# Pieces of 256 and 320 tokens instead of 320 and 256 in the first two batches of a fused attention and squared-relu layer

## The chip, the cores and the metric

The kernel runs on one core of a Trainium2 chip. The metric is the device time of one execution in microseconds (us); less is better. A core has five engines with queues of their own, each of which runs its instructions strictly in its order: TensorE (PE: matmuls, with PEld for loading their weights), VectorE (DVE), ScalarE (ACT), GpSimd (POOL) and SyncE (SP). They wait for each other through semaphores. Transfers between the main memory and the core's memory are issued by POOL and SP here, and run on 16 DMA engines. Matmuls write to PSUM, eight banks of 2 KB per partition; ACT and DVE read it from there.

## The reference

```python
def sm_attn(qq, kk, vv):
    s = scale * np.matmul(qq, kk.transpose(0, 1, 3, 2))
    s = s - np.max(s, axis=-1, keepdims=True)
    a = np.exp(s)
    a = a / (np.sum(a, axis=-1, keepdims=True) + 1e-09)
    return np.matmul(a, vv)
p_packed = sm_attn(p, k, v)
out = sm_attn(q, p_packed, p_packed)
...
x = np.ascontiguousarray(attn_out.transpose(0, 2, 1, 3)).reshape(B * S, H * D)
h = x @ w_in
r = np.maximum(h, 0.0)
g = r * r
return (g @ w_out).astype(np.float32)
```

There are 8 batches of 8 heads, 576 tokens and a head size of 64; p has 32 rows per head. So the first attention packs 576 rows of k and v into 32 rows (softmax one, over 576), and the second one lets 576 rows of q look at those 32 (softmax two, over 32). What comes out, 4608 tokens of 512 values, passes a first layer of 512 x 2048, a relu that is squared, and a second layer of 2048 x 512. Everything is float32 outside; the kernel computes in bfloat16 with float32 sums.

## The kernel before, in words

Nothing here is ordered by a compiler or a planner at build time. One long text, `ORDER` (L50), names every step as a word, and `run` (L770) issues the steps in that order; each step puts its instructions at the end of its engine's queue. A letter behind a colon gives the engine where there is a choice: `v` is DVE, `a` ACT, `p` POOL. DVE is meant where none is given.

The heads of a batch are worked on as two quads, 0 and 1. With b for the batch and q for the quad, the words of one batch are, in the order in which they depend on each other:

- `Lkbq`, `Lvbq`, `Lq`/`LA`/`LB`: loads of k, v and q, issued by POOL (L270, L310 and others). In batches 0 and 1, q comes in two parts, A and B. `Wi`, `Wo`: the two weights, in pieces, also by POOL. POOL's loads have eight semaphores in turn, so that a load waits until the eighth one before it has landed, and what stands behind it on POOL waits too. `pf`, `P0`, `P1`: p of the first two batches, loaded by SP, cast and turned by DVE (L233, L237).
- `kT` (DVE, L353) turns k; `s1` (PE, L377) gives the scores of softmax one; `m1` its maximum (DVE, L403); `x1` the exponential (ACT, L415); `eT` turns it on PE (L435), `eo` copies that out of PSUM; `rd`, `pv` (PE, L459) and `pp` (DVE, L472) make the packed rows; `bd` (DVE) and `pt`, `po` turn them for the next two uses.
- `qT`, or `qA` and `qB` (DVE, L365): q turned. `s2`, or `zA` and `zB` (PE, L377): scores of softmax two. `t2`/`tA`/`tB` (DVE, L520): turned out of PSUM so that 32 neighbours are one row; `m` maximum (L525); `s` difference (L531); `x` exponential (ACT, L537); `u` sum and reciprocal (DVE, L543, L545); `a` product with it (L551); `aT`/`TA`/`TB` (DVE, L565): turned for the first layer.
- `w0`, `w1`, and in batch 0 `wa` and `wb` for the halves of `w0` (PE, L576): the packed rows times the first layer's weights, so that the first layer is applied to the 32 packed rows once, and each token needs only its mixture of them. `W..` (L421, L423): copied out of PSUM.
- `hb.p.f` (PE, L592): the first layer of batch b, piece p of its tokens, block f of 16 blocks of 128 features: two matmuls, one for each quad, into one bank. `r` (ACT L597, DVE L599): relu out of that bank. `qb.p.f`, with f up to 7 (DVE L637, ACT L635, POOL): the square, two blocks at once, into `gT`.
- `ot.j` (PE, L650): the second layer of 128 tokens (t is 0 to 35), two of its 16 matmuls at a step. `c` copies the 128 x 512 result out of PSUM, `d` stores it (SP, L681).
- `Zn` (L337): n matmuls of 288 columns of zeros, of which nothing is used. They stand only in the first stretch, where PE has nothing else to do.

PSUM is shared out by hand: two double banks (`psa`) for scores, turns and `w`; four more, first as three `spare` and one `idle`, then, from the first `h` on, as two `x` and two `y`. A step that takes one of two buffers waits for the reader of the step before the last that took it. In batch 0, `h` of an even block takes `x`, of an odd block `y`; the `o` of the first two token tiles takes `y`, later ones `x`.

Batches 2 to 7 pass softmax two in one go and the first layer in halves of 288. Batches 0 and 1 pass both in the two pieces that `CUTS` gives:

```python
PIECES = range(2)
HALVES = ((0, HALF), (HALF, S))
CUTS = ((0, 320), (320, S))
...
def part(self, b, hf):
    return (CUTS if b in PIECES else HALVES)[hf]
...
def span(self, hf):
    s0, s1 = (0, S) if hf is None else CUTS[hf]
    return slice(s0 // NP, s1 // NP)
```

So `h0.0.f` and `zA0` work on the first piece, `h0.1.f` and `zB0` on the second. Token tiles 0 and 1 (tokens 0 to 255) lie within the first piece, tiles 2 and 3 (256 to 511) reach into or lie in the second.

Of the kernel before, what the change touches and what calls it, by code (L numbers as in the profile page):

```python
# [24 lines left out]
S = T * NP  # L25
# [14 lines left out]
CUTS = ((0, 320), (320, S))  # L40
# [10 lines left out]
pf Lk00 Lk01 Lv00 LA0 Lv01 Wi11 P0 Wi10 kT00 I Z30 s100 Wi00 LB0 kT01 P1 Wi01 m100 Z7 s101 Wi21 x100 m101 x101 Z6 eT00  # L51
Wi20 qA01 Z4 eT01 qA00 eo00:a eo01:v Lk10 rd0 Z5 pv0 pp0 bd0 Z4 pt0 Lk11 zA0 po0:v tA01 tA00 Z12 wb00 mA01 Wb00:a mA00
Z2 wb01 sA01:p Wb01:v Wo0 sA00:v xA01 uA01 xA00 Lv11 qB00 qB01 aA01:p uA00 Z21 zB0 Lv10 tB01 Z1 wa00 tB00 aA00:p mB01
Wa00:a Z3 wa01 TA01 mB00 Wa01:a sB01:p TA00 sB00:v Z8 h0.0.8 xB01 h0.0.1 xB00 r0.0.8:v h0.0.0 Wo2 r0.0.1:a h0.0.3 uB01
r0.0.0:a h0.0.10 uB00 h0.0.11 aB01:p r0.0.10:a h0.0.2 r0.0.3:a q0.0.0:v r0.0.2:a h0.0.9 r0.0.11:v aB00:p q0.0.1:a TB01
w101 LA1 q0.0.5:v r0.0.9:a w100 TB00 W101:a W100:v h0.1.0 q0.0.4:p h0.1.1 h0.1.11 r0.1.0:a h0.1.10 r0.1.1:a kT10
h0.1.2 r0.1.10:a LB1 h0.1.3 r0.1.11:a h0.0.12 r0.1.2:a q0.1.0:v h0.1.15 r0.1.3:a q0.1.5:p h0.0.4 r0.0.12:v r0.1.15:a
h0.0.13 kT11 r0.0.4:a h0.1.6 h0.0.5 r0.0.13:a Wo1 h0.0.6 q0.1.1:v r0.1.6:a h0.1.13 q0.0.6:v r0.0.5:a s11 r0.1.13:v Wo3
q0.0.2:a r0.0.6:v h0.1.14 m110 h0.1.7 r0.1.14:a h0.1.12 Pr h0.1.9 r0.1.7:a h0.1.4 q0.1.7:v r0.1.12:a h0.0.15 r0.1.9:v
x110 h0.0.14 r0.1.4:v h0.0.7 m111 r0.0.15:a h0.1.8 eT10 r0.0.14:a r0.1.8:v h0.1.5 r0.0.7:a o2.0 eo10:v q0.1.3:a o3.0  # L60
r0.1.5:v x111 q0.0.3:v o1.0 q0.1.2:v o0.0 q0.1.4:a q0.0.7:v o0.1 rd1 q0.1.6:p eT11 o1.1 eo11:v o3.1 pv1 Lk20 o0.2 pp1
o1.2 bd1 o3.2 o1.3 qA10 pt1 qA11 o0.3 o3.3 po1:v zA1 qB11 w011 tA11 o2.1 W011:a tA10 o2.2 qB10 o2.3 mA11 mA10 w110
w111 sA11 o3.4 Lk21 W110:a sA10 o1.4 W111:v o0.4 xA11 o0.5 xA10 uA11 zB1 w010 tB11 o1.5 uA10 o1.6 aA11 W010:a o0.6
mB11 o1.7 aA10 o2.4 Px TA11 Lk30 c1:v o3.5 o0.7 TA10 sB11 o3.6 kT20 d1 c0:a h1.0.8 Lv20 o2.5 r1.0.8:a Pt h1.0.3 xB11
h1.0.6 tB10 d0 r1.0.3:a o2.6 Pu:v h1.0.1 r1.0.6:a Lv21 o2.7 r1.0.1:a kT21 h1.0.0 c2:a h1.0.2 o3.7 r1.0.0:a uB11 Lv30
d2 r1.0.2:a s12 q1.0.0:v c3:a h1.0.4 mB10 o4.0 m120 q1.0.1:a Lq2 h1.0.5 d3 o5.0 r1.0.4:a m121 r1.0.5:a o5.1 aB11 x120
h1.0.12 q1.0.2:v h1.0.7 o4.1 kT30 Lq3 x121 eT20 o4.2 TB11 r1.0.12:a r1.0.7:v o5.2 sB10 eo20:a h1.0.13 rd2 q1.0.3:v
eT21 xB10 r1.0.13:v h1.0.9 eo21:a o4.3 r1.0.9:v h1.0.15 q1.0.6:a uB10 pv2 q1.0.4:v h1.0.10 pp2 o5.3 Lv31 r1.0.15:a
r1.0.10:v o4.4 aB10 pt2 h1.0.14 bd2 h1.0.11 po2:v r1.0.14:a o5.4 bs2:v r1.0.11:a w121 TB10 w020 q1.0.5:v W121:a h1.1.8
q1.0.7:v h1.1.9 o4.5 W020:v o5.5 r1.1.8:a r1.1.9:a o4.6 Lv40 h1.1.4 qT21 h1.1.6 r1.1.4:a o5.6 q1.1.4:a qT20 o4.7 Lk31  # L70
r1.1.6:a h1.1.2 o5.7 c4:v h1.1.14 r1.1.2:a s22 c5:a r1.1.14:v h1.1.10 t221 o6.0 d5 r1.1.10:a h1.1.1 t220 o6.1 r1.1.1:a
h1.1.7 m221 o6.2 d4 h1.1.0 r1.1.7:a o6.3 qT30 r1.1.0:a h1.1.5 q1.1.3:a h1.1.3 q1.1.0:v Lq4 o6.4 qT31 r1.1.5:a o6.5
q1.1.2:a sb21:v h1.1.13 r1.1.3:a o8.0 m220 r1.1.13:a h1.1.11 o6.6 q1.1.1:a Lq5 r1.1.11:v o6.7 x221 sb20:v h1.1.15 o8.1
c6:a q1.1.5:v h1.1.12 x220 su21 d6 o7.0 r1.1.12:a Lk41 w120 r1.1.15:a w021 kT31 q1.1.6:a o7.1 q1.1.7:a o8.2 su20
W120:a o7.2 o8.3 a221 W021:a o7.3 a220 o8.4 o7.4 aT21 o8.5 aT20 o7.5 h2.0.2 h2.0.3 r2.0.2:v o7.6 Lk40 r2.0.3:a o8.6
q2.0.1 o7.7 h2.0.1 h2.0.0 r2.0.1:v o8.7 r2.0.0:a c7:v s13 c8:a q2.0.0 h2.0.7 d7 h2.0.6 m130 Lk50 r2.0.7:a o9.0
r2.0.6:a h2.0.4 m131 o10.0 d8 r2.0.4:a h2.0.9 q2.0.3 x131 h2.0.5 r2.0.9:v o10.1 r2.0.5:v x130 o9.1 kT41 h2.0.12
h2.0.10 r2.0.12:a q2.0.2 eT31 Lk51 r2.0.10:a eT30 rd3 h2.1.1 eo31:v h2.0.8 r2.1.1:a o9.2 kT40 r2.0.8:a h2.1.0 eo30:a
o9.3 r2.1.0:v h2.0.11 Lk60 q2.0.4 pv3 q2.1.0 r2.0.11:a h2.1.3 pp3 o10.2 r2.1.3:a q2.0.5 h2.0.13 bd3 o10.3 bs3:v
r2.0.13:a Lv41 h2.1.5 h2.0.14 r2.1.5:v s23 q2.0.6 o9.4 qT40 r2.0.14:a h2.0.15 o9.5 t231 r2.0.15:a h2.1.4 h2.1.8 q2.0.7  # L80
o10.4 Lv51 r2.1.8:a t230 o9.6 r2.1.4:a o10.5 m231 h2.1.7 h2.1.2 q2.1.2 o9.7 r2.1.7:a qT41 r2.1.2:a o10.6 c9:a sb31:v
h2.1.11 Lq6 h2.1.14 r2.1.11:a d9 o11.0 q2.1.1 h2.1.6 m230 r2.1.14:a o11.1 r2.1.6:a o10.7 x231 sb30:v h2.1.10 h2.1.12
q2.1.3 pt3 r2.1.10:a o11.2 c10:v po3:a h2.1.9 r2.1.12:a su31 w030 x230 w130 d10 o11.3 r2.1.9:a q2.1.5 W030:a o12.0
q2.1.4 h2.1.13 su30 o12.1 W130:a o11.4 a231 o12.2 r2.1.13:a w131 a230 w031 o12.3 W031:a aT31 o11.5 aT30 h2.1.15 W131:v
o12.4 r2.1.15:a h3.0.0 h3.0.11 r3.0.0:a o12.5 q2.1.6 q2.1.7 r3.0.11:a h3.0.1 s14 r3.0.1:v h3.0.3 kT51 h3.0.7 r3.0.3:a
o11.6 r3.0.7:a m140 h3.0.10 o11.7 r3.0.10:a q3.0.0 h3.0.8 x140 kT50 h3.0.2 o12.6 r3.0.8:a c11:v o12.7 Lk61 r3.0.2:a
h3.0.14 q3.0.5 h3.0.5 d11 m141 o14.0 r3.0.14:a c12:a eT40 q3.0.1 h3.0.4 r3.0.5:a o13.0 x141 r3.0.4:v Lk71 h3.1.9 d12
eo40:v o14.1 r3.1.9:a q3.0.2 o13.1 h3.0.12 rd4 h3.0.6 o13.2 r3.0.12:v r3.0.6:a o14.2 h3.0.13 q3.0.3 h3.1.8 eT41
r3.0.13:v o13.3 r3.1.8:a eo41:v h3.0.9 q3.0.6 h3.0.15 o14.3 q3.1.4 r3.0.9:a r3.0.15:v pv4 q3.0.4 h3.1.5 Lv50 pp4
h3.1.6 r3.1.5:a q3.0.7 o14.4 bd4 o13.4 bs4:v r3.1.6:a pt4 Lv60 o14.5 h3.1.1 h3.1.0 po4:v r3.1.1:a o14.6 r3.1.0:v  # L90
h3.1.14 q3.1.0 w041 r3.1.14:a w141 o14.7 W141:v h3.1.3 W041:a h3.1.2 o13.5 o13.6 r3.1.2:a r3.1.3:v c14:a s24 q3.1.1
h3.1.7 h3.1.4 t240 r3.1.7:a o15.0 d14 r3.1.4:a o13.7 t241 h3.1.10 c13:a o15.1 q3.1.3 r3.1.10:a h3.1.12 q3.1.2 o17.0
m240 r3.1.12:a o17.1 d13 m241 h3.1.11 h3.1.13 r3.1.11:a o15.2 sb40:v r3.1.13:a h3.1.15 o15.3 q3.1.5 r3.1.15:a sb41:v
o17.2 x240 o17.3 q3.1.7 o15.4 x241 q3.1.6 su40 w140 w040 o15.5 W040:a su41 o17.4 o15.6 W140:a a240 o17.5 o15.7 a241
s15 c15:a aT40 o17.6 aT41 o16.0 m150 d15 h4.0.4 h4.0.10 kT60 r4.0.4:a o16.1 r4.0.10:a h4.0.0 m151 x150 o17.7 Lk70
h4.0.1 r4.0.0:v o16.2 x151 qT50 o16.3 r4.0.1:a h4.0.3 c17:v eT50 r4.0.3:a h4.0.2 q4.0.0 eo50:a o16.4 d17 r4.0.2:v
h4.0.7 rd5 qT51 o18.0 r4.0.7:a h4.0.11 q4.0.1 o16.5 Lq7 r4.0.11:a kT61 h4.0.6 h4.0.5 o18.1 r4.0.6:a q4.0.5 o16.6
r4.0.5:a q4.0.3 h4.0.13 q4.0.2 h4.0.12 r4.0.13:v eT51 o16.7 eo51:v r4.0.12:a h4.0.15 o18.2 q4.0.6 r4.0.15:a h4.0.9
c16:v h4.1.0 o18.3 r4.0.9:a r4.1.0:v d16 pv5 h4.1.1 Lv61 h4.0.8 o19.0 pp5 r4.1.1:a o19.1 r4.0.8:v h4.0.14 Lv70 q4.1.0
h4.1.3 bd5 r4.0.14:a pt5 o19.2 q4.0.4 bs5:a po5:v h4.1.2 r4.1.3:v o18.4 r4.1.2:a q4.0.7 h4.1.5 q4.1.1 h4.1.15 o18.5  # L100
r4.1.5:v o18.6 r4.1.15:a h4.1.10 h4.1.4 s25 r4.1.10:v r4.1.4:a o18.7 qT61 h4.1.8 c18:a h4.1.7 t251 o19.3 o20.0 q4.1.2
r4.1.8:a d18 o19.4 r4.1.7:a m251 h4.1.6 h4.1.14 t250 o19.5 r4.1.6:a o20.1 sb51:v r4.1.14:a h4.1.9 q4.1.3 w150 r4.1.9:a
w151 m250 x251 h4.1.13 o19.6 W150:v r4.1.13:a o20.2 W151:a o19.7 sb50:v h4.1.12 c19:a h4.1.11 w050 su51 w051 d19 x250
o20.3 r4.1.11:a q4.1.4 o21.0 W050:a q4.1.7 o21.1 q4.1.5 o20.4 su50 r4.1.12:a o21.2 W051:a o21.3 q4.1.6 o20.5 a250
o20.6 a251 o21.4 o20.7 aT50 aT51 s16 qT60 o21.5 c20:a h5.0.1 m160 h5.0.0 r5.0.1:a o21.6 r5.0.0:a m161 h5.0.3 d20
h5.0.2 r5.0.3:a o21.7 q5.0.0 x160 r5.0.2:v h5.0.4 o22.0 kT71 c21:a h5.0.7 eT60 r5.0.4:a q5.0.1 o23.0 r5.0.7:a kT70 d21
x161 h5.0.11 h5.0.5 eo60:v o22.1 r5.0.11:a r5.0.5:v eT61 rd6 h5.0.15 eo61:v o23.1 r5.0.15:a h5.0.9 q5.0.2 pv6 r5.0.9:v
# [29 lines left out]
class Kernel:  # L137
# [184 lines left out]
# [4 lines that stand above are left out]
# [64 lines left out]
    def st_s2(self, b, hf=None):  # L390
# [3 lines left out]
        for qd in range(self.NQ):  # L394
            t = self.att[b, qd]
            ps = t["ps_s2", hf] = self.turn32("ps_s2") if hf is None else one[:, qd:qd + 1]
            x.append((ps, t["ppd"], t["qT"], [(h, self.group(qd, h)) for h in range(QH)]))
        self.scores(HALVES if hf is None else CUTS[hf:hf + 1], x)

# [425 lines left out]
```

## Time and profile before

| what | us |
|---|---|
| median of three runs (243.95 to 244.98) | 244.84 |
| the profiled execution | 243.8 |
| span of the profile, first to last instruction | 242.0 |
| busy in it: TensorE, VectorE, ScalarE, GpSimd | 236.4, 206.3, 138.2, 75.9 |
| first useful first-layer matmul / first second-layer matmul | 21.89 / 33.52 |
| last matmul's result ready to be copied | 234.00 |
| mean relu of 256, 288, 320 elements on ACT | 0.390, 0.411, 0.442 |
| the same on DVE | 0.418, 0.453, 0.481 |
| mean square of 512, 576, 640 elements on DVE | 0.399, 0.443, 0.512 |
| mean square of 512, 640 elements on ACT | 0.638, 0.746 |

A profile shows one execution. Its times are counted from the first instruction, and its span is shorter than the execution's time by what lies before and after, 1.8 us here. A row's mean is the length of one instruction from start to end; where an engine works without a pause, the next starts some hundredths of a us before the one ahead has ended, so that n instructions take a little less than n means. "Start to start" below means that shorter distance.

### The profile page before, as it was taken

How to read it: one execution, taken by the hardware profiler on the slowest of the kernel's cores; microseconds unless marked ns; L12 is line 12 of the kernel's file. 1: busy time of each engine (PE TensorE's matmuls, PEld its weight loads, DVE VectorE, ACT ScalarE, POOL GpSimd, SP SyncE). 2: the span in 40 equal slices, each digit the busy share in tenths (PEclk: the TensorE clock that was granted, in tenths of full speed). 3: DMA queues.
4: the chain of work that ended last, by engine and by line, in shares of the span. 5: the costliest groups of instructions: out<-in, count | busy, mean ns of one | idle time of the engine just before them, and what ended most of it. 6: DMA issues, size and time to landing. Idle time of an engine off the chain costs nothing.

```text
span 242.0 us, 6193 instructions
## 1 busy us (share of the span) xinstructions
PE 236.4 (98%) x2459; PEld 130.5 (54%) x2459; DVE 206.3 (85%) x455; ACT 138.2 (57%) x310; POOL 75.9 (31%) x125
## 2 busy tenths in 40 slices
PE   8999999999999999999999999999999999999994
PEld 5766564445554565455554655456544645555543
DVE  2679996999998899998899988997999899976830
ACT  2325981588787666864576645875584569523300
POOL 8657962783575394051401440002000000000000
PEclk9999999999999999999999999999999999999999
DMA  6999999999999979726831796125032121211214
GB/s 104 198 199 209 204 207 201 158 153 258 199 196 208 207 118 128 160 35 154 97 90 43 118 164 99 43 54 84 4 87 48 44 46 24 65 43 43 51 40 128
DMA packets 33404, 28.51 MB, mean 118 GB/s; under 512 B 8160, under 2 KB 28384, under 8 KB 33376
## 3 DMA queue, kind: packets, MB, share of 16 engines
q0 software_dynamic: 26848, 18.55, 54.0%
q1 hardware_dynamic: 6384, 9.51, 14.9%
q8 instruction: 19, 0.31, 0.5%
q10 hardware_dynamic: 144, 0.07, 0.1%
q14 instruction: 9, 0.07, 0.1%
HBM read 37.22 MB, written 9.44 MB: 193 GB/s over the span
## 4 chain that ended last, share of the span: by engine, by line
PE 89%; ACT 3%; DVE 2%; POOL 1%; issue 1%; DMA 1%; SPq 1%; ACTq 0%; POOLq 0%
PE ps_o L650 50%; PE ps_h L592 25%; PE ps_idle L337 4%; PE ps_wp L576 3%; PE ps_s L377 3%; ACT r L597 2%; PE ps_e1T L435 2%; PE ps_pv L459 1%; DMA out_dram<-o_sb 1%; SPq L681 1%; POOL gT L310 1%; POOL a L551 1%; PE ps_ppT L498 0%; ACT wp L421 0%; ACT e L415 0%
## 5 line engine op out<-in xcount | busy, mean ns | idle before, releaser
L650 PE MATMUL ps_o<-w_out_bf,gT 128*128 128x512 bf16 (+1 forms) x576 | 149.0, 378 | 0.0
L597 ACT ACTIVATE r<-ps_h 128x288 bf16<-128x288 f32 (+2 forms) x181 | 68.9, 412 | 55.4 <-PE ps_h L592 54.9
L592 PE MATMUL ps_h<-a2T,wp 128*128 128x288 bf16 (+2 forms) x512 | 89.6, 286 | 1.2 <-ACT r L597 0.5
L650 PEld LDWEIGHTS <-gT 128*128 128x128 bf16 x576 | 54.3, 98 | 42.1 <-issue 3.6
L592 PEld LDWEIGHTS <-wp 128*128 128x128 bf16 x512 | 48.1, 98 | 42.1 <-issue 7.0
L637 DVE TENSOR_TENSOR gT<-r 128x576 bf16<-128x576 bf16 (+2 forms) x113 | 48.2, 447 | 2.9 <-ACT r L597 2.4
L599 DVE TENSOR_SCALAR r<-ps_h 128x288 bf16<-128x288 f32 (+2 forms) x75 | 33.2, 453 | 11.6 <-PE ps_h L592 10.3
L421 ACT CAST wp<-ps_wp 128x1024 bf16<-128x1024 f32 (+1 forms) x24 | 22.6, 962 | 16.2 <-PE ps_wp L576 16.1
L270 POOL DMA_DIRECT2D k_b<-in_k_dram x28 | 15.2, 545 | 38.2 <-DVE kT L353 27.2
L315 POOL DMA_DIRECT2D v_b<-in_v_dram x12 | 9.5, 793 | 32.8 <-PE ps_pv L459 32.7
L337 PE MATMUL ps_idle<-gT 128*128 128x288 bf16 x103 | 17.2, 321 | 1.1 <-DVE gT L189 1.1
L421 ACT COPY o_sb<-ps_o 128x512 f32<-128x512 f32 x22 | 12.9, 587 | 8.3 <-PE ps_o L650 8.2
L415 ACT ACTIVATE e<-ps_s,nm 128x576 bf16<-128x576 f32 x16 | 11.9, 750 | 7.8 <-DVE nm L403 7.7
L353 DVE STREAM_TRANSPOSE kT<-k_b 128x576 uint32<-128x576 uint32 x16 | 12.3, 770 | 3.0 <-DMA k_b<-in_k_dram 3.0
L270 POOL DMA_DIRECT2D q_b<-in_q_dram x16 | 11.0, 695 | 8.6 <-DVE qT L365 6.4
L337 PEld LDWEIGHTS <-gT 128*128 128x128 bf16 x103 | 10.4, 109 | 5.7 <-DVE gT L189 1.1
L365 DVE STREAM_TRANSPOSE qT<-q_b 128x576 uint32<-128x576 uint32 (+2 forms) x20 | 12.4, 634 | 0.3 <-PE ps_s L377 0.2
L423 DVE CAST wp<-ps_wp 128x1024 bf16<-128x1024 f32 (+1 forms) x10 | 11.6, 1161 | 1.1 <-PE ps_wp L576 1.0
L543 DVE TENSOR_REDUCE sums<-e 128x18 f32<-128x576 f32 (+2 forms) x20 | 12.2, 610 | 0.0
L537 ACT ACTIVATE e<-d 128x576 f32<-128x576 f32 (+2 forms) x20 | 11.4, 586 | 1.2 <-POOL d L531 0.8
L403 DVE TENSOR_REDUCE nm<-ps_s 128x1 f32<-128x576 f32 x16 | 11.6, 737 | 0.6 <-PE ps_s L377 0.6
L525 DVE TENSOR_REDUCE mx<-s 128x18 f32<-128x576 f32 (+2 forms) x20 | 11.9, 612 | 0.0
(60 smaller groups left out, 191.6 us busy)
## 6 DMA issues: line engine op xcount, KB each, us to landing
out_dram<-o_sb SPq DMA_DIRECT2D x65, 128.0 KB, 2.7
v_b<-in_v_dram POOLq DMA_DIRECT2D x12, 256.0 KB, 5.3
w_out_bf<-in_moe_w_out_dram POOLq DMA_DIRECT2D x4, 512.0 KB, 13.0
q_b<-in_q_dram POOLq DMA_DIRECT2D x6, 288.0 KB, 6.2
q_b<-in_q_dram POOLq DMA_DIRECT2D x12, 144.0 KB, 6.5
k_b<-in_k_dram POOLq DMA_DIRECT2D x12, 108.0 KB, 3.9
gT<-in_v_dram POOLq DMA_DIRECT2D x4, 288.0 KB, 10.5
w_in_bf<-in_moe_w_in_dram POOLq DMA_DIRECT2D x4, 256.0 KB, 10.4
```

The lines of the kernel that those rows point to most:

```text
L270: engine.dma_start(x[n:], s[:P - n])
L337: self.nc.tensor.matmul(ps[:, :HALF], lhsT=self.nought[:, :P], rhs=self.nought, start=True, stop=True)
L353: self.nc.vector.transpose(t["kT"][:].rearrange("p s e -> p (s e)").bitcast(U32), t["k"][:].rearrange("p t d -> p (t d)").bitcast(U32))
L365: self.nc.vector.transpose(out.bitcast(U32), x.bitcast(U32))
L415: self.nc.scalar.activation(out, x, ACT.Exp, bias=t["nm"], accum_out=self.den[b][:, qd:qd + 1])
L421: engine.copy(out, x)
L543: nc.vector.reduce_sum(out=sums[:, x], in_=t["e2"][:, x], axis=AX.X)
L592: self.nc.tensor.matmul(ps, lhsT=t["wp"][:, fb // n, fb % n * P:(fb % n + 1) * P], rhs=t["a2T"][:, s0:s1], start=(qd == 0), stop=(qd == se ...
L597: engine.activation(r, ps, ACT.Relu)
L599: engine.tensor_scalar_max(r, ps, 0.0)
L637: engine.tensor_tensor(out=out, in0=r, in1=r, op=ALU.mult)
L650: self.nc.tensor.matmul(self.o[tt][:, e], lhsT=self.gT[:, fb, a:a + P], rhs=self.w_out_bf[:, fb, e], start=(i == 0), stop=(i == self.NFB - 1))
```

## The change

The cut between the two pieces of batches 0 and 1 goes from token 320 to token 256, so that the first piece is the smaller one. With it, the whole `ORDER` is another one: the same steps in another sequence, with another share between the engines and 105 idle matmuls instead of 103. Counted over the text:

| step | before | after |
|---|---|---|
| relus on ACT / DVE | 181 / 75 | 159 / 97 |
| of these in batch 0 | 23 / 9 | 20 / 12 |
| squares on DVE / ACT / POOL | 113 / 12 / 3 | 104 / 21 / 3 |
| copies of `w` products on ACT / DVE | 21 / 9 | 26 / 4 |
| copies of results on ACT / DVE | 22 / 14 | 26 / 10 |
| differences and products of softmax two on POOL (batch 0) | 2 and 4 | 1 and 3 |

The diff, cut to the line of the cut and to the order as far as the first steps of the second layer:

```diff
-CUTS = ((0, 320), (320, S))
+CUTS = ((0, 256), (256, S))
...
-pf Lk00 Lk01 Lv00 LA0 Lv01 Wi11 P0 Wi10 kT00 I Z30 s100 Wi00 LB0 kT01 P1 Wi01 m100 Z7 s101 Wi21 x100 m101 x101 Z6 eT00
-Wi20 qA01 Z4 eT01 qA00 eo00:a eo01:v Lk10 rd0 Z5 pv0 pp0 bd0 Z4 pt0 Lk11 zA0 po0:v tA01 tA00 Z12 wb00 mA01 Wb00:a mA00
-Z2 wb01 sA01:p Wb01:v Wo0 sA00:v xA01 uA01 xA00 Lv11 qB00 qB01 aA01:p uA00 Z21 zB0 Lv10 tB01 Z1 wa00 tB00 aA00:p mB01
-Wa00:a Z3 wa01 TA01 mB00 Wa01:a sB01:p TA00 sB00:v Z8 h0.0.8 xB01 h0.0.1 xB00 r0.0.8:v h0.0.0 Wo2 r0.0.1:a h0.0.3 uB01
-r0.0.0:a h0.0.10 uB00 h0.0.11 aB01:p r0.0.10:a h0.0.2 r0.0.3:a q0.0.0:v r0.0.2:a h0.0.9 r0.0.11:v aB00:p q0.0.1:a TB01
-w101 LA1 q0.0.5:v r0.0.9:a w100 TB00 W101:a W100:v h0.1.0 q0.0.4:p h0.1.1 h0.1.11 r0.1.0:a h0.1.10 r0.1.1:a kT10
...
-x110 h0.0.14 r0.1.4:v h0.0.7 m111 r0.0.15:a h0.1.8 eT10 r0.0.14:a r0.1.8:v h0.1.5 r0.0.7:a o2.0 eo10:v q0.1.3:a o3.0
...
+pf Lk00 Lk01 Lv00 Lv01 I P0 LA0 P1 Wi00 kT00 Wi10 LB0 Z32 s100 Wi01
+kT01 Wi11 m100 Z4 s101 x100 m101 Wi21 x101 Z13 eT00 eo00:v Z2 eT01 rd0 eo01:v
+Wi20 Z4 pv0 pp0 qA01 Lk10 Z4 pt0 bd0 qA00 po0:a Z5 zA0 Lk11 tA00 tA01
+mA01 mA00 sA01:v xA01 sA00:v uA01 xA00 qB00 Wo0 qB01 aA01:p uA00 Z33 zB0 wa00 Lv11
+tB00 tB01 aA00:p Wa00:a mB00 Z5 wa01 mB01 sB00:p Wa01:a TA01 Z3 wb01 TA00 Lv10 wb00
+xB00 sB01:v h0.0.8 h0.0.9 Wb01:a Wb00:v h0.0.1 h0.0.0 xB01 uB00 r0.0.8:a r0.0.1:a h0.0.2 uB01 r0.0.9:a aB00:p
+r0.0.0:a h0.0.3 r0.0.2:v q0.0.4:a h0.0.11 Wo2 aB01:v h0.0.10 q0.0.0:a TB00 TB01 r0.0.3:a r0.0.10:v r0.0.11:a h0.1.0 h0.1.1
+q0.0.1:v q0.0.5:a h0.1.9 r0.1.0:v h0.1.8 r0.1.1:a r0.1.9:v LA1 w100 w101 q0.1.0:v r0.1.8:a h0.1.10 W100:v W101:a h0.1.11
...
+r0.0.6:a Wo3 h0.1.15 q0.0.7:v q0.0.6:a h0.0.7 r0.1.15:v h0.1.4 r0.0.7:a Lv20 h0.1.6 m110 r0.1.4:a h0.1.5 r0.1.6:a h0.1.7
+m111 h0.1.12 q0.0.3:a o2.0 x110 r0.1.5:v o2.1 r0.1.12:v q0.1.7:p o0.0 x111 o3.0 r0.1.7:a eT10 q0.1.6:a o0.1
...
```

## What the change should do to the time: the prediction

> **What bounds the kernel now.** I read the page first, then the windows by stage, TensorE's timeline of the first 36 us, the chain of waits behind it, then the other engines' timelines there. On the page, TensorE (PE) is busy 98% of the span and slices 2 to 39 all show a 9; VectorE (DVE) is close behind, ScalarE (ACT) not.
>
> ```profile
> PE 236.4 (98%) x2459; PEld 130.5 (54%) x2459; DVE 206.3 (85%) x455; ACT 138.2 (57%) x310; POOL 75.9 (31%) x125
> ...
> PE   8999999999999999999999999999999999999994
> ...
> DVE  2679996999998899998899988997999899976830
> ACT  2325981588787666864576645875584569523300
> ```
>
> The windows (us; busy time and instructions of each engine) show where that average lies. From 34 on TensorE is full: the end is then the start of its full stretch, plus work, plus a tail. From 22 to 34 ACT is busy 11.61 of 12 us and DVE 11.41; there they are the limit.
>
> ```profile
> 0.00:22.00 22.00, 20.86 (x278) 13.56 (x279) 13.77 (x38) 6.32 (x11) 15.28 (x28) 1.00 1.13 174
> 22.00:34.00 12.00, 10.96 (x138) 7.34 (x136) 11.41 (x27) 11.61 (x31) 9.90 (x14) 1.00 1.23 207
> 34.00:50.00 16.00, 16.00 (x181) 7.06 (x180) 13.71 (x36) 6.69 (x12) 9.19 (x16) 1.00 1.25 177
> ```
>
> TensorE's timeline (start, length, what, count) shows the same from its side. Before 21.89 it fills waits with idle matmuls (L337). The first-layer matmuls (L592) start at 21.89; the second layer (L650) at 33.52, after which the row is never again short of work for longer than 0.4 us.
>
> ```profile
> 16.66 2.75 PE L337 MATMUL ps_idle<-gT 128*128 128x288 bf16 x21
> ...
> 21.89 2.06 PE L592 MATMUL ps_h<-a2T,wp 128*128 128x320 bf16 x14
> ...
> 25.80 3.90 PE L592 MATMUL ps_h<-a2T,wp 128*128 128x256 bf16 x28 [0.45 <-DVE a2T L565]
> ...
> 33.52 2.32 PE L650 MATMUL ps_o<-w_out_bf,gT 128*128 128x512 bf16 x10
> ```
>
> The chain of waits has the undisturbed rates: four 320-column matmuls in 0.54 (0.136 each), four of 256 in 0.44 (0.109), and the last matmuls up to 234.00.
>
> ```profile
> 55.25 0.54 PE ps_h L592 x4
> ...
> 69.35 0.44 PE ps_h L592 x4
> ...
> 230.94 3.04 PE ps_o L650 x14
> 234.00 0.70 DVE o_sb L423
> ```
>
> From 21.89 to 33.52 there are 11.63 us. Work in it: 32 matmuls x 0.136 + 32 x 0.109 + w101/w100 0.56 + s11 0.65 + eT10 0.34 = 9.4. So 2.2 us are waits on the relus, about all that TensorE loses between its first real work and the tail. What the change is worth is decided before 34 us.
>
> **The change, part by part.** The multiset of steps is the same; what moves is sizes, engines, places and idle matmuls (103 to 105).
>
> *Up to the first scores.* DVE casts and turns batch 1's p (P1) ahead of the first k. Its last p load lands at 5.89, so kT00 runs 6.5 to 7.25 instead of 5.73 to 6.51. Idle matmuls cover it: Z32 for Z30 adds 2 x 0.127 (21 take 2.67 start to start), and s100 is due at 7.64 (7.38). Without that cover it would cost up to 0.8. Z4 for Z7 brings s101 to 8.86 (8.97).
>
> *Softmax one.* Z13 for Z6: eT00 at 11.08 (10.33), eT01 11.70 (11.39); both copies out now on DVE, the second 12.27 to 12.82; pp at 13.28 (13.10). Both qA transposes (pairs of 256: 0.30 start to start) now stand behind pp: zA0 at 14.70 (13.86), +0.84.
>
> *First piece of softmax two, 256 for 320.* On DVE: two turns 0.70, two maxima 0.60, both subtractions 0.82 (one was GpSimd's, 0.74), exp 0.41, sum and reciprocal 0.6: first factor ready 18.1, second 19.5. GpSimd issues Wo0's load (it waits for qB; by its kilobytes that lands at 17.2) until 18.2, multiplies 18.25 to 19.0, issues Lv11, multiplies to 20.45. It was 21.45: the first piece is 1.0 us ahead here.
>
> *It does not reach TensorE.* 33 idle matmuls, 4.16 us, put zB0 at 19.26 (19.33), and on DVE the two zB turns (0.84) and maxima (0.84), now 320 wide, stand ahead of TA01 and TA00: from 19.80 to 21.48, then TA until 21.96. wb00 waits for the copy Wa01 (wa01 waits for the turns to free its PSUM, 20.75; copy to 21.71). So h0.0.8 starts at 22.02: **+0.13**. No load is late: in the order of bytes Wi01 lands near 18.6, Wi11 near 19.8, before wa00 (19.7) and wb01 (21.5).
>
> *Relus and squares until o2.0.* ACT's timeline gives the steps: 5 relus of 320 in 1.84 (0.37), 11 of 256 in 3.45 (0.31), a 640-element square 0.65 start to start (a 512 one, by its shorter mean 0.638 against 0.746, 0.55), a wp copy 0.90.
>
> ```profile
> 22.70 1.84 ACT L597 ACTIVATE r<-ps_h 128x320 bf16<-128x320 f32 x5
> 24.57 0.74 ACT L635 ACTIVATE gT<-r 128x640 bf16<-128x640 bf16 x1
> ...
> 25.53 1.00 ACT L421 CAST wp<-ps_wp 128x1024 bf16<-128x1024 f32 x1
> 26.43 3.45 ACT L597 ACTIVATE r<-ps_h 128x256 bf16<-128x256 f32 x11
> ```
>
> After: xB00 21.88, Wb01, xB01, then the first relu at 23.13. From there to the relu r0.1.4, whose bank h0.1.12 needs: 10 of 256 (3.1), 8 of 320 (2.9), 5 squares of 256 (2.75), one of 320 (0.65), W101 (0.9) with a wait of 0.15 for w101: 10.5, so 33.6; o2.0 also needs the next relu's bank: 34.0 to 34.3, taken 34.2 (**+0.7** on 33.52). Cross-check by differences: ACT has 4 relus fewer there (-1.4), 4 squares (+2.3) and Wb01 (+0.5) more, x110 falls behind (-0.7): +0.7. DVE, with 12 of the 32 relus (9 before), ends as late: its m111 is done near 34.3. Queued behind ACT's squares are the relus that free the banks; TensorE waits for them, and its h work is 9.05 of these 12.2 us.
>
> *What is still owed.* At 33.52 eT10 was done; now it follows o2.0: **+0.34**. From there each o step is 0.43 and all its inputs are ready, so TensorE is full.
>
> *Batch 1.* Its attention starts 2 to 3 us later (m110 near 33 instead of 30.96) and runs beside o0 to o3. DVE from pp1 (38.7) to TA11, 24 instructions with one W copy, takes 10.2 us by steps, with waits until 49.9; TensorE's own row reaches h1.0.1 at 49.9. A tie; before, the chain of waits passes there through a relu of 0.45 at 49.82. I take 0.1 more, between 0 and 1.5.
>
> *Loads.* GpSimd's squares hold back Wo1's issue from 28.7 to about 30.5; the queue still has the loads that landed up to 38.3 ahead of it, so it lands near 40.8 as before and is used near 44.6. Nothing; without that backlog, up to 1.8.
>
> *Rest.* 11 relus more on DVE in batches 2 to 7, four output copies and five wp copies fewer there: by means DVE's total falls (22 x 0.45 against 9 x 0.44 + 5 x 1.2 + 4 x 0.68, and 0.9 from GpSimd: about -2). TensorE's work is the same but for 0.25 of idle matmuls, counted above. I take nothing, bounds -0.4 (the one long wait gone) to +1 (one later stage that loses about what the relu stage does).
>
> Sum: 0.13 + 0.55 in the relu stage (0.7 at o2.0) + 0.34 + 0.1 = **+1.1** on the span of 242.0, so about 243.1; the profiled execution was 243.8 with 1.8 around its span and stands 1.0 below the median 244.84. On the median: **246.0**.
>
> A pair of rows shows one thing more: DVE's square of 640 took 0.68 while GpSimd multiplied (23.57 to 25.0), and 0.45 once it was done.
>
> ```profile
> 23.85 0.68 DVE L637 TENSOR_TENSOR gT<-r 128x640 bf16<-128x640 bf16 x1
> ...
> 25.08 0.45 DVE L637 TENSOR_TENSOR gT<-r 128x640 bf16<-128x640 bf16 x1
> ```
>
> Three two-input steps now lie within 0.4 of a GpSimd one (sB01, aB01, q0.1.0); at 0.23 each that is up to 0.7, on DVE, which is not first to end there: none taken. The Trainium skill (SBUF — State Buffer, "two separate sides") says that a VectorE step with two SBUF inputs and a GpSimd step take one port pair in turn, the loser blocked for the whole instruction. The two rows agree in kind; by the rule a blocked step would lose up to GpSimd's whole 1.27 us rather than 0.23, and 247.3 would be the time if one such block fell on the last relu before o2.0; that case is counted with the late rival below.
>
> **The rivals.**
> *Faster: the relu waits close.* The second piece's matmul pair is 0.27 instead of 0.22 while a relu of 320 costs ACT only 0.06 more; if DVE's extra relus keep the banks free, the 2.2 us of waits vanish: 0.13 + 0.34 - 2.2 = -1.7, 243.1. It decides once ACT's r0.1.4 ends before about 32. For it: the two DVE queues end together, so both share. Against: ACT was full there and gets 0.7 more.
> *Batch 1 late.* If DVE's 24 steps take their mean lengths (11.7) and not the steps, TA11 is 1.5 later and TensorE, which has run out of o steps, waits: 247.5. For: the tie. Against: idle matmuls apart, such a wait occurs once before, under 0.45.
> *Nothing.* The stage loses 0.7 but that 0.4 wait and some 0.1 us changes of shape later fall away, eT10 hides in a wait: 244.8 to 245.2.
>
> **How the numbers follow.** What can't be told from no change is 0.5%, here 243.6 to 246.1. Forecast (245.3 to 246.8) 0.50, of which 0.28 lies above 246.1; batch 1 or a later stage late 0.24, all above; nothing 0.12; faster 0.14, of which 0.12 lies below 243.6. Faster 0.12, same 0.36, slower 0.52. The range runs from the faster rival's 243.1 to 248.6, the late rival with the rest's +1.
>
> **What would show it.** zB0 at 19.3 and the first L592 at 22.0; the first L650 at 34.2 with ACT full from 23; o2.0 ahead of eT10; TensorE at h1.0 near 50 with a wait under 0.5; the last L650 ending near 235.1. I am wrong if the first L650 starts before 33, or if TensorE has waits of over 0.5 after 36.

## The result: 0.35% faster, where slower was forecast

| kernel | median us (lowest to highest, runs) | ratio to before, 95% interval |
|---|---|---|
| before | 244.12 (243.69 to 244.98, 7) | |
| after | 243.41 (242.95 to 243.46, 7) | 0.9965 [0.995, 0.9979] |

The kernel became 0.7 us faster, within the 0.5% that the prediction called no change. The forecast of 246.0 had the wrong sign. A ratio, here and below, compares a kernel with runs of the kernel before that were taken alongside it (in the experiments their medians were 243.95 to 244.07), so it is not the quotient of two medians on this page.

The page of after, the rows that answer to those of before (line numbers of after are 8 higher):

```profile
PE 235.7 (98%) x2461; PEld 130.8 (54%) x2461; DVE 203.3 (84%) x459; ACT 142.0 (59%) x308; POOL 74.7 (31%) x123
...
PE   8999899999999999999999999999999999999994
...
DVE  2679986999998789989998889997899879987650
ACT  2216993697898567956693647774495346733300
```

Work went from DVE (206.3 to 203.3) and POOL to ACT (138.2 to 142.0), as the step counts say. TensorE's share did not move (98%): the kernel is bound as before. The windows by stage of after (us; busy time and instructions of PE, PEld, DVE, ACT, POOL, then clock, DMA share, GB/s):

```profile
0.00:22.00 22.00, 20.69 (x283) 14.06 (x284) 13.85 (x39) 5.64 (x12) 14.26 (x27) 1.00 1.13 173
22.00:34.00 12.00, 10.72 (x130) 6.63 (x129) 11.57 (x27) 11.82 (x31) 9.39 (x12) 1.00 1.23 207
34.00:50.00 16.00, 16.00 (x186) 7.35 (x185) 12.87 (x37) 9.47 (x18) 8.77 (x16) 1.00 1.35 185
```

In the relu stage (the window from 22 to 34) ACT is busier (11.82 for 11.61) and TensorE less busy (10.72 for 10.96); the stage was not repaired. TensorE's timeline of after (start, length, what, count) dates it:

```profile
14.43 0.42 PE L385 MATMUL ps_s<-qT,ppd 32*32 32x256 bf16 x16
14.78 4.22 PE L345 MATMUL ps_idle<-gT 128*128 128x288 bf16 x33
18.93 0.47 PE L385 MATMUL ps_s<-qT,ppd 32*32 32x320 bf16 x16
...
21.61 1.03 PE L600 MATMUL ps_h<-a2T,wp 128*128 128x256 bf16 x8
23.23 1.20 PE L600 MATMUL ps_h<-a2T,wp 128*128 128x256 bf16 x8 [0.58 <-DVE rs L553]
24.78 1.56 PE L600 MATMUL ps_h<-a2T,wp 128*128 128x320 bf16 x8 [0.35 <-DVE a2T L573]
...
28.37 2.54 PE L600 MATMUL ps_h<-a2T,wp 128*128 128x256 bf16 x18 [0.29 <-ACT r L605]
...
33.34 1.92 PE L658 MATMUL ps_o<-w_out_bf,gT 128*128 128x512 bf16 x8
```

From these rows and TensorE's last ones the change of the profiled executions (243.8 and 243.41 us; spans 242.0 and 241.6) is put together:

| stage of TensorE | before | after | difference |
|---|---|---|---|
| first layer starts | 21.89 | 21.61 | -0.28 |
| relu stage, until the second layer starts | 11.63 | 11.73 | +0.10 |
| from there to the start of the last first-layer matmul | 197.14 | 196.89 | -0.25 |
| last matmul ends | 238.8 | 238.3 | -0.4 |

How much of a row a single execution can move is seen from the runs below. Five profiles have the new order's rest with both cuts at 256: their third row is 196.89 to 196.93. Four of them have the relu stage of after unaltered: their second row is 11.72 or 11.73. The first row is less firm: a second profile of the kernel after starts the first layer at 21.42, so -0.28 is known to some 0.2 only.

In the third row 0.34 is owed for eT10, which now lies behind that start; for equal work the rest of the kernel is 0.59 shorter. One piece of that is plain. In before, TensorE at h1.0.1 waits for a relu:

```profile
49.66 0.43 PE L592 MATMUL ps_h<-a2T,wp 128*128 128x320 bf16 x2
50.31 0.43 PE L592 MATMUL ps_h<-a2T,wp 128*128 128x320 bf16 x2 [0.21 <-ACT r L597]
```

Two such matmuls take 0.27 start to start; here 0.65 pass, so 0.37 is lost. In after, the same stage goes by fours without a gap (4 x 0.109 and 4 x 0.216 are what these rows have between starts):

```profile
49.14 0.60 PE L600 MATMUL ps_h<-a2T,wp 128*128 128x256 bf16 x4
49.57 1.03 PE L658 MATMUL ps_o<-w_out_bf,gT 128*128 128x512 bf16 x4
50.44 0.60 PE L600 MATMUL ps_h<-a2T,wp 128*128 128x256 bf16 x4
```

### The profile page after: what moved, and what is told of

Its sections match the earlier page's. It is cut to its first block, busy times and chain, and to the rows that moved or that the text cites. A ratio compares the mean times of both kernels' runs of the same rounds, so it can differ in the third digit from the quotient of the medians.

```text
span 241.6 us, 6190 instructions
## 1 busy us (share of the span) xinstructions
PE 235.7 (98%) x2461; PEld 130.8 (54%) x2461; DVE 203.3 (84%) x459; ACT 142.0 (59%) x308; POOL 74.7 (31%) x123
## 4 chain that ended last, share of the span: by engine, by line
PE 94%; ACT 2%; DMA 2%; DVE 1%; SPq 0%; issue 0%; ACTq 0%; DVEq 0%
PE ps_o L658 52%; PE ps_h L600 26%; PE ps_idle L345 4%; PE ps_wp L584 4%; PE ps_s L385 3%; PE ps_e1T L443 2%; DMA gT<-in_p_dram 2%; PE ps_pv L467 1%; ACT r L605 1%; ACT gT L643 0%; PE ps_ppT L506 0%; ACT wp L429 0%; PE ps_o L663 0%; DVE kT L361 0%; SPq L278 0%; ACT e L545 0%
## 5 line engine op out<-in xcount | busy, mean ns | idle before, releaser
L658 PE MATMUL ps_o<-w_out_bf,gT 128*128 128x512 bf16 (+1 forms) x576 | 147.3, 378 | 0.0
L605 ACT ACTIVATE r<-ps_h 128x288 bf16<-128x288 f32 (+2 forms) x159 | 61.0, 415 | 47.2 <-PE ps_h L600 43.9
L607 DVE TENSOR_SCALAR r<-ps_h 128x288 bf16<-128x288 f32 (+2 forms) x97 | 41.8, 446 | 11.2 <-PE ps_h L600 10.6
L645 DVE TENSOR_TENSOR gT<-r 128x576 bf16<-128x576 bf16 (+2 forms) x104 | 45.1, 445 | 2.8 <-ACT r L605 1.8
L429 ACT CAST wp<-ps_wp 128x1024 bf16<-128x1024 f32 (+1 forms) x29 | 27.7, 974 | 9.1 <-PE ps_wp L584 9.0
L429 ACT COPY o_sb<-ps_o 128x512 f32<-128x512 f32 x26 | 15.2, 589 | 12.3 <-PE ps_o L658 11.9
L278 POOL DMA_DIRECT2D q_b<-in_q_dram x16 | 10.9, 684 | 29.9 <-DVE qT L373 25.4
L345 PE MATMUL ps_idle<-gT 128*128 128x288 bf16 x105 | 16.7, 314 | 1.1 <-DVE gT L197 1.1
L643 ACT ACTIVATE gT<-r 128x512 bf16<-128x512 bf16 (+1 forms) x21 | 14.0, 689 | 0.5 <-DVE r L607 0.3
```

Source lines behind the costliest of these rows:

```text
L278: engine.dma_start(x[n:], s[:P - n])
L345: self.nc.tensor.matmul(ps[:, :HALF], lhsT=self.nought[:, :P], rhs=self.nought, start=True, stop=True)
L429: engine.copy(out, x)
L605: engine.activation(r, ps, ACT.Relu)
L607: engine.tensor_scalar_max(r, ps, 0.0)
L643: engine.activation(out, r, ACT.Square)
```

## The experiments

Two things changed at once, a cut and an order. All times below are medians; "second scores" is the second PE row of 24 matmuls in the first 10 us (s101), and "rest" the time from the first second-layer matmul to the last first-layer one.

**The new order with the old cut.**

```diff
-CUTS = ((0, 256), (256, S))
+CUTS = ((0, 320), (320, S))
```

> The changed kernel with the cut put back to 320 and its order left as it is. If the smaller first piece itself is what made it faster, this one loses the gain: 244.1 or more, with the first first-layer matmul 0.3 to 0.8 us later than 21.61. If the order made it faster, it stays within 0.4 us of 243.4, and the relu stage (first first-layer to first second-layer matmul) stays at 11.5 to 12.0 us.

Measured: 244.14 us, ratio 1.0006 [0.9993, 1.0018]. The first layer starts at 21.82, the second at 33.74, the rest is 197.21. Against before, the relu stage is 0.29 longer (11.92) and the rest 0.07, with eT10's 0.34 in it. The order alone gains nothing that can be measured. The first layer starts 0.21 later than in after, less than the 0.3 to 0.8 that was expected of the cut.

**The old order with batch 0 cut at 256** (batch 1 stays at 320).

```diff
-CUTS = ((0, 320), (320, S))
+CUTS = {0: ((0, 256), (256, S)), 1: ((0, 320), (320, S))}
```

> The kernel before with batch 0 alone cut at 256 (batch 1 stays at 320, because the old order passes token tile 6 before the second piece of batch 1), order as it was. If the cut is the gain: 243.4 to 243.7. If the order is: 243.9 to 244.6, since 30, 12 and 21 idle matmuls and the load of the first layer's weights set the start of the first layer, whatever the cut.

Measured: 244.74 us, 1.003 [1.0011, 1.0048]. TensorE's timeline shows what the new cut meets in the old order:

```profile
24.24 0.38 PE L592 MATMUL ps_h<-a2T,wp 128*128 128x256 bf16 x2 [0.23 <-ACT r L597]
25.48 0.62 PE L576 MATMUL ps_wp<-w_in_bf,ppT 64*32 64x512 bf16 x16 [0.86 <-DMA w_in_bf<-in_moe_w_in_dram]
...
34.49 1.67 PE L650 MATMUL ps_o<-w_out_bf,gT 128*128 128x512 bf16 x7
```

The second layer starts 1.0 later than in before. Of this, 0.33 is there when the first layer starts (22.22). The largest loss is the 0.86 before w101: TensorE comes to it at 24.62, 0.1 sooner than in before (24.73), and its weights land at 25.4. In before the same load landed at 24.7, just in time; it moves between executions (24.4 with the old head and the new rest, 25.1 in the run with the wait filled, where TensorE waits 0.40 for it). So most of the 0.86 is this execution's load and not the cut. The twelve runs are 0.3% slower, a little more than was expected if the order were the gain (243.9 to 244.6): in the old order, batch 0's cut brings nothing, and what it costs apart from the load stays open. Batch 1's cut was not tried there.

**Each order's head with the other's rest.** The text of one kernel up to the second layer's start, with the other's text behind it; steps that would be missing or doubled are put at the seam. The new head has batch 0 cut at 256 and batch 1 at 320, the old head both at 320.

> The changed kernel's order up to the first second-layer step, then everything that is left in the old order (batch 0 cut at 256, batch 1 at 320). If the gain is made before that step (first-layer start 0.28 us earlier, relu stage 0.10 longer, eT10 owed): first second-layer matmul at 33.3 to 33.4 and time 243.4 to 243.8. If it is made behind it (the wait of 0.37 us at h1.0 and the changes of shape that fell away): 243.9 to 244.3, with that wait at h1.0 back.

> The old order up to the first second-layer step, then everything left in the new order (cut at 320 in both batches). The mirror image: 243.9 to 244.3 if the gain is made in the head, 243.4 to 243.7 if it is made in the rest, with no wait over 0.2 us at h1.0.

Measured: new head, old rest 245.36 us, 1.0051 [1.0036, 1.0067]; old head, new rest 243.83, 0.9993 [0.9975, 1.0011]. The first is slower than either case that was expected, for a reason of the seam, as its TensorE row shows:

```profile
31.49 2.02 PE L606 MATMUL ps_h<-a2T,wp 128*128 128x320 bf16 x14
35.23 0.54 PE L449 MATMUL ps_e1T<-ident,e 128*96 128x128 bf16 x6 [1.72 <-ACT e L429]
35.60 1.67 PE L664 MATMUL ps_o<-w_out_bf,gT 128*128 128x512 bf16 x7
```

It keeps eT10 ahead of o2.0, and the exponential that eT10 turns comes late there: on ACT it stands behind a square of the new head and two relus that were put at the seam. TensorE waits 1.72 us. It therefore says nothing of the old rest, and its 1.72 is not the price of eT10's place. But in after too that exponential ends at 34.5, 1.2 after o2.0 starts: in the new head, eT10 has to stand behind o2.0. The second run is clean: with eT10 at its old place and the old cut, the rest takes 196.85 against 197.14, with a wait of 0.16 in place of 0.37. The new order of the rest alone is worth 0.29 in the profile; the medians can't tell it from nothing, as its head starts the second layer at 33.61, 0.09 later than before's.

**The one wait of before, filled.** h1.0.6 goes from in front of o2.6 to behind it, so that TensorE has work while the relu runs.

```diff
-h1.0.6 tB10 d0 r1.0.3:a o2.6 Pu:v h1.0.1
+tB10 d0 r1.0.3:a o2.6 h1.0.6 Pu:v h1.0.1
```

> The kernel before with one step moved: h1.0.6 stands behind o2.6 on TensorE, so that o2.6 fills the wait of 0.37 us for the relu r1.0.8. If TensorE is full from 34 us to the end, so that each wait costs its own length: 0.3 to 0.4 us faster than the kernel before, and the last first-layer matmul at about 230.3 instead of 230.66. If the wait is given back by later ones: within 0.1 us.

Measured: 243.64 us, 0.9995 [0.9983, 1.0007]: not told from before. TensorE loses the time one pair of matmuls later:

```profile
50.40 1.00 PE L592 MATMUL ps_h<-a2T,wp 128*128 128x320 bf16 x4
51.24 0.59 PE L650 MATMUL ps_o<-w_out_bf,gT 128*128 128x512 bf16 x2
```

0.84 for what takes 0.54, so 0.30 of the 0.37 is back, and the rest is 197.06 against 197.14. The second relu stands behind an exponential on ACT in both orders; moving the matmul only moves where TensorE meets it.

**Batch by batch.** The kernel after with one batch cut at 320 again.

```diff
-CUTS = ((0, 256), (256, S))
+CUTS = {0: ((0, 256), (256, S)), 1: ((0, 320), (320, S))}
```

and, in the second run, the two entries exchanged.

> The kernel after with only batch 1 cut at 320 again (batch 0 at 256, the new order throughout). Theory, each cut pays where it stands: head and relu stage are batch 0's and stay as in the kernel after (first layer starts at 21.3 to 21.6, second layer about 11.7 us later), and all of the 0.3 us that the old cut of both batches cost behind the second layer's start comes back (197.2 us from there to the last first-layer matmul instead of 196.9, with a wait of about 0.16 us near 53.7): about 243.7 us. Rival, only batch 0's cut matters: the rest stays at 196.9 us, about 243.4 us, not to be told from the kernel after.

> The kernel after with only batch 0 cut at 320 again (batch 1 at 256, the new order throughout). Theory, each cut pays where it stands: the first layer starts about 0.2 us later than in the kernel after (21.8), the relu stage takes about 0.2 us more (11.9), and the rest is as in the kernel after (196.9 us, no wait near 53.7): about 243.8 us. Rival, only batch 0's cut matters: all of the old cut's loss appears here, the rest at 197.2 us, about 244.1 us.

| kernel (new order) | median us, ratio | first layer | second layer | rest |
|---|---|---|---|---|
| both at 256 (after) | 243.41, 0.9965 [0.995, 0.9979] | 21.61 | 33.34 | 196.89 |
| batch 1 at 320 | 243.80, 0.9991 [0.9977, 1.0005] | 21.65 | 33.37 | 197.25 |
| batch 0 at 320 | 243.76, 0.9990 [0.9977, 1.0002] | 21.80 | 33.70 | 196.87 |
| both at 320 | 244.14, 1.0006 [0.9993, 1.0018] | 21.82 | 33.74 | 197.21 |

The two cuts add up: batch 0's is worth 0.36 before the second layer starts and nothing behind it, batch 1's 0.36 behind it and nothing ahead. Executions can move the head by as much, but here the second scores of all four lie within 0.03 (8.74 to 8.77), and the medians agree: one cut put back costs 0.35 or 0.39, both cost 0.73. Single steps of TensorE show that all of batch 1's share is spent between 44 and 76, where batch 1's first layer lies. No single wait makes it. The longest is one of 0.16 in the kernel with batch 1 at 320 (the second row below ought to take 0.54 and the next one starts 0.70 on), but after loses 0.10 at the same step (0.54 for 0.44, in the last two rows), so that it accounts for 0.06. What the other 0.30 is made of stays open. First the kernel with batch 1 at 320, then after:

```profile
52.53 1.03 PE L658 MATMUL ps_o<-w_out_bf,gT 128*128 128x512 bf16 x4
53.40 0.70 PE L600 MATMUL ps_h<-a2T,wp 128*128 128x320 bf16 x4
54.10 1.04 PE L658 MATMUL ps_o<-w_out_bf,gT 128*128 128x512 bf16 x4
```

```profile
53.04 0.60 PE L600 MATMUL ps_h<-a2T,wp 128*128 128x256 bf16 x4
53.58 1.04 PE L658 MATMUL ps_o<-w_out_bf,gT 128*128 128x512 bf16 x4
```

**The kernel after again, and a square of it on GpSimd.** If ACT alone is the limit of the relu stage, a square taken from it shortens the stage.

```diff
-r0.0.0:a h0.0.3 r0.0.2:v q0.0.4:a h0.0.11 Wo2 aB01:v h0.0.10 q0.0.0:a TB00
+r0.0.0:a h0.0.3 r0.0.2:v q0.0.4:a h0.0.11 Wo2 aB01:v h0.0.10 q0.0.0:p TB00
```

> The changed kernel unaltered, as the measure for the other three of this group. Either the 0.7 us of the first medians (0.43 in the two profiles) is the same again: 243.2 to 243.6 beside 243.9 to 244.1 of the kernel before; or part of it was the draw of few runs: nearer than 0.4 us to the kernel before.

> The changed kernel with one square of batch 0 (q0.0.0) on GpSimd instead of ScalarE, 0.52 us of ScalarE's time start to start. If ScalarE sets the relu stage: the first second-layer matmul 0.4 to 0.5 us earlier than 11.73 us after the first first-layer one, and the time 0.4 us shorter. If VectorE or the chain through the PSUM banks sets it: no change within 0.1 us, and more idle time on ScalarE.

Measured: the kernel after 243.34 us, 0.9975 [0.9965, 0.9986]; with the square on GpSimd 243.65, 0.9989 [0.9978, 1.0001]. The intervals overlap, but in the profile the stage takes 12.01 instead of 11.72. GpSimd's row, then DVE's, of that run:

```profile
24.52 1.05 POOL L645 TENSOR_TENSOR gT<-r 128x512 bf16<-128x512 bf16 x1
```

```profile
24.59 0.38 DVE L607 TENSOR_SCALAR r<-ps_h 128x256 bf16<-128x256 f32 x1
24.90 0.96 DVE L645 TENSOR_TENSOR gT<-r 128x512 bf16<-128x512 bf16 x1
```

The same square of DVE takes 0.43 in after, where GpSimd is not multiplying. Here it ends 0.3 after GpSimd's does, as if it had done its work once GpSimd was done. The relu beside it, which reads PSUM, took its usual 0.38. The Trainium skill (SBUF — State Buffer, "two separate sides") has a VectorE step with two SBUF inputs blocked for the whole GpSimd instruction; the 0.96 agrees. So does the pair of rows that the prediction took for a milder case, at 0.23: the first of the two GpSimd products there runs from 23.57 to 24.18, and the square that began at 23.85 ended at 24.53, 0.35 after it. It lost less because less of the product was left. TensorE then waits 0.68 for DVE's copy of `wp`: ACT was helped by 0.5 and DVE hurt by as much, and the stage got longer. ACT is not its only limit; by how much a square less on ACT would shorten the stage if DVE were left alone, this run can't show.

**The idle matmuls and the place of P1.** Do the first 9 us set the start of the first layer?

```diff
 before, fewer idle matmuls:
-kT00 I Z30 s100
+kT00 I Z22 s100
 after, P1 behind kT01, fewer idle matmuls (third run: Z32 kept):
-LA0 P1 Wi00 kT00 Wi10 LB0 Z32 s100 Wi01
-kT01 Wi11
+LA0 Wi00 kT00 Wi10 LB0 Z22 s100 Wi01
+kT01 P1 Wi11
```

> The kernel before with 22 instead of 30 idle matmuls ahead of the first scores. In the profiles so far the first idle matmuls took 5.5 to 6.5 us for 30 to 32 of them, so that the first scores come at 6.6 or at 7.5 without any change of data. If that, passed down through fixed counts of idle matmuls, sets the start of the first layer and spreads the runs of the kernel before (243.2 to 245.4): scores at 6.6 in each run, first layer 0.2 to 0.3 us earlier, limited then by the weights' load that lands at 19.6, the spread under 1 us. If loads set it anyhow: first layer at 21.8 to 22.0 and the same time and spread.

> The changed kernel with p of batch 1 (P1) cast behind the second k, as in the old order, and 22 instead of 32 idle matmuls ahead of the first scores. In four profiles of the new head the first layer starts 14.1 us after the first scores, and these wait for the first k, which stands on VectorE behind P1 (its last load lands at 5.9). If that is what paces the new head: first scores at 6.6 instead of 7.0 to 7.5, first layer at 20.9 to 21.1 (the second scores need the second k at 8.1 to 8.3), and 242.7 to 243.0. If a load or VectorE's later queue paces it, as in the old head: first layer at 21.4 or later, time unchanged.

> The same with the 32 idle matmuls kept. If these cover P1, as the prediction had it, the first scores stay at 6.6 to 7.5, set by the idle matmuls alone (5.4 to 6.3 us by when TensorE gets quick), and the time lies between 242.9 and 243.4. If P1's place alone is the cost, this one is as quick as the other.

| kernel | median us, ratio | second scores | first layer | between |
|---|---|---|---|---|
| before | 244.12 | 8.97 | 21.89 | 12.92 |
| before, fewer idle | 244.52, 1.0017 [1.0003, 1.0031] | 8.51 | 22.37 | 13.86 |
| before, wait filled (the same head) | 243.64, 0.9995 [0.9983, 1.0007] | 8.21 | 21.89 | 13.68 |
| after | 243.41, 0.9965 [0.995, 0.9979] | 8.74 | 21.61 | 12.87 |
| after again | 243.34, 0.9975 [0.9965, 0.9986] | 8.55 | 21.42 | 12.87 |
| after, P1 late, Z22 | 243.20, 0.9974 [0.9952, 0.9996] | 8.31 | 21.30 | 12.99 |
| after, P1 late, Z32 | 243.50, 0.9973 [0.9957, 0.9988] | 8.96 | 21.84 | 12.88 |

In the new head the first layer follows the second scores at a distance of 12.9 to 13.0 us in each of these profiles. In the old head it does not: scores that come 0.5 or 0.8 earlier gain nothing, because TensorE then meets a load, as its row in the run with fewer idle matmuls shows:

```profile
16.32 0.30 PE L576 MATMUL ps_wp<-w_in_bf,ppT 64*32 64x256 bf16 x8 [0.52 <-DMA w_in_bf<-in_moe_w_in_dram]
```

That this run starts the first layer later than before does, and not at the 21.8 to 22.0 expected of a head bound by loads, is the load's doing: it landed at 16.3 here and at 15.6 in before. So the old head was held by its weights' loads and the new one, which asks for them in another order, by the chain of computations. Moving P1 back gave 0.1 to 0.3 in the profile (21.30 against 21.42 and 21.61, where 20.9 to 21.1 was expected) and nothing that the medians can tell from the kernel after. With Z32 kept, the scores came later than the 6.6 to 7.5 expected, because the idle matmuls lasted until 7.8 in that execution. No version here beats the kernel after for sure.

## Why the prediction was wrong, point by point

Its sum was 0.13 + 0.55 + 0.34 + 0.1 = +1.1 on the span. By the same places the profiles have -0.28, +0.10, +0.34 and -0.59, together -0.43. Three of the four terms failed, and the largest miss, 0.69, is batch 1 with the rest: the prediction gave batch 1's own cut no gain. The other 1.0 us between 246.0 and 243.41 is its base: more runs put the median of before at 244.12 instead of 244.84 (0.7), and the profiled execution of before stands 0.3 below that, the one of after at its median.

- **First layer at 22.02 (+0.13): failed, 0.41 us, and ahead of the step that was argued.** "It does not reach TensorE" held: GpSimd's last product of the first piece ends at 20.04 in after and at 20.89 in the kernel with batch 0 at 320, and DVE's turns that need it start at 21.07 and 21.04, behind the maxima, as the prediction had it. GpSimd's and DVE's rows of after, then of the other:

```profile
19.41 0.63 POOL L559 TENSOR_TENSOR a<-e,rs 128x256 bf16<-128x256 f32 x1
21.07 0.49 DVE L573 STREAM_TRANSPOSE a2T<-a 128x128 uint32<-128x128 uint32 x2
```

```profile
20.15 0.74 POOL L559 TENSOR_TENSOR a<-e,rs 128x320 bf16<-128x320 f32 x1
21.04 0.56 DVE L573 STREAM_TRANSPOSE a2T<-a 128x160 uint32<-128x160 uint32 x2
```

  The steps that failed are "Up to the first scores" and "Softmax one". The second scores came at 8.74 for 8.86, and zA0 at 14.43 for 14.70; 33 idle matmuls pass that on, zB0 came at 18.93 for 19.26, and the last 0.08 fell behind it. The 0.12 at the scores is the execution's luck (8.55 in a second profile of after). The cut has a share by the same path, which the prediction put at nothing: at the same second scores (8.74) zA0 starts at 14.43 with the cut at 256 and at 14.54 with 320, because DVE's two turns of q ahead of it are narrower (0.43 and 0.40 for 0.50 and 0.47); it is also shorter, so that zB0 starts 0.17 earlier and the first layer 0.19 (21.61 and 21.80).
- **"Relus and squares until o2.0": right direction, mis-sized, 0.45 us.** ACT did take more work, and TensorE's stage did grow, by 0.10 instead of 0.55. The ACT steps were too long. They were had by dividing a row's length by its count, with the last instruction's overhang in it. Also, the row "11 of 256 in 3.45" is eight relus of 256 and three of 320, and two of its steps lasted 0.36 and 0.39 where the other relus of 256 took 0.26 or 0.27. ACT's timeline of after:

```profile
22.81 1.19 ACT L605 ACTIVATE r<-ps_h 128x256 bf16<-128x256 f32 x4
23.86 1.18 ACT L643 ACTIVATE gT<-r 128x512 bf16<-128x512 bf16 x2
24.90 0.68 ACT L605 ACTIVATE r<-ps_h 128x256 bf16<-128x256 f32 x2
...
27.88 1.38 ACT L605 ACTIVATE r<-ps_h 128x320 bf16<-128x320 f32 x4
29.10 0.77 ACT L643 ACTIVATE gT<-r 128x640 bf16<-128x640 bf16 x1
```

  From row start to row start, four relus of 256 take 1.05, or 0.26 each where the forecast had 0.31; two squares of 512 take 1.04, or 0.52 where it had 0.55; and the last relus, three of 320 and one of 256, take 1.22, which leaves 0.32 for one of 320 where it had 0.37. (Such a relu of 256 is 0.39 long, so the next one starts 0.13 before its end: more than "some hundredths".) With these steps the forecast's own list adds up to 9.3 and not 10.3. But the stretch from r0.0.8 to the end of r0.1.4, forecast at 10.5 from 23.13, took 10.1 from 22.81: ACT waited some 0.7 in it, where the forecast had 0.15. So two errors partly cancelled. o2.0 followed 0.4 later, not 0.6. That the stage hangs on ACT alone fell with these waits and with the square on GpSimd.
- **"What is still owed", eT10: right.** It follows o2.0, at 35.09, and takes 0.34 there.
- **"Batch 1" and "Rest": failed, 0.69 us.** Batch 1 was in time: TensorE reaches h1.0 at 49.14 and waits for nothing. The rest was taken at 0 between -0.4 and +1. It is -0.59 for equal work: 0.29 from the order (old head, new rest) and 0.32 to 0.36 from batch 1's cut, a term that the prediction left out: it priced the cut in batch 0 alone. The 0.37 wait was seen, in the bounds of the rest and in the rival "Nothing", and left out of the sum.
- **Idle matmuls as cover for P1: partly.** s100 came at 7.52, forecast 7.64, but after a wait of 0.23 for kT, so the cover was already gone in this execution; in the two batch-by-batch runs it waits 0.67 and 0.84.
- **The rivals.** None is what happened. "Faster" named the right sign and 243.1, by way of relu waits that close; they did not (TensorE is busy 10.72 of 12 us there, 10.96 before). Its sum was -1.7 where the profiles have -0.43, and that 243.1 lies near 243.41 is luck: the base was 1.0 too high. "Nothing" named the right places, the owed eT10 and the 0.4 wait, with the relu stage's loss still in it.
- **A misreading.** The table of before gives 234.00 for the last matmul's result. The chain of waits leaves TensorE there for the copy of an earlier token tile; TensorE's own row runs until 238.8, so the sign "the last L650 ending near 235.1" could not have come true. The last copy waits for the last matmuls in both kernels; in before the chain shows a store that lands at 238.81, which ties with them, and in after it shows the matmuls:

```profile
230.27 0.24 PE ps_h L600 x2
230.52 6.92 PE ps_o L658 x36
237.43 0.91 PE ps_o L663 x16
```

## What to carry to other kernels

Read an engine's own pace from a row in which nothing held it up, from start to start, and see that the row holds one shape only; a row's length divided by its count, in a stage where the engine waits for another, prices every added instruction too high. When a size is changed in several batches, price it in each: here the second one was worth as much as the first, and lay where TensorE had seemed full. Try a cut and an order apart and together: here the order alone was worth nothing that could be measured, batch 0's cut in the old order cost 0.3%, and both cuts in the new order gained 0.35%. And where a weight is used just as it lands, one profile's wait for it says little: the same load landed up to 1.0 us apart.

## What was not expected of the hardware

The first idle matmuls step at 0.240 us and later ones at 0.123, and the moment of the turn differs from execution to execution: between 3.86 and 6.55 us in the twelve profiles that show it, with the first matmul at 1.07 or 1.08 each time. TensorE's first row of two runs, 32 matmuls each (the kernel after with P1 late, then the one with batch 0 at 320):

```profile
1.08 6.74 PE L345 MATMUL ps_idle<-gT 128*128 128x288 bf16 x32 [1.08 <-DVE gT L197]
```

```profile
1.07 5.61 PE L345 MATMUL ps_idle<-gT 128*128 128x288 bf16 x32 [1.07 <-DVE gT L197]
7.53 0.69 PE L385 MATMUL ps_s<-kT,pT 32*32 32x192 bf16 x24 [0.84 <-DVE kT L361]
```

Thus a count of idle matmuls is a poor clock: the same 32 end 1.1 us apart in these two, and whether they cover a late input is a matter of the execution. The windows' clock column says 1.00 throughout, so only the steps show it. The Trainium skill (TensorE: Matmul & The Clock Gate, "Part 1: The HAM clock gate") says that the gate opens after about 3.4 us of work by a window that runs freely and does not start with the kernel; that the turn moves agrees, but its ±0.5 us is too little for the 2.7 us spread here, and the measurement decides.
